# Spectral filter and Mish MLP on one core: low row parts turned by transposing transfers, w1 scaled in four parts, another order in the opening, a last tile in three pieces, joined row-0 products

## The chip, the core and the metric

The kernel runs on one core of a Trainium2 chip. The metric is the device time of one execution in microseconds. The core has TensorE (PE in the profile; its weight loads PEld), VectorE (DVE), ScalarE (ACT), GpSimd (POOL), and SyncE (SP), which issues the transfers. They run apart from each other, each through its own queue in order, and wait for each other by semaphores.

## The reference

```python
xn = layernorm(x)                                   # x: 2048 rows of 512, f32
h = xn @ w1 + b1                                    # w1: 512 x 1792
mlp = (h * tanh(softplus(h))) @ w2                  # mish; w2: 1792 x 512
X = rfft2(xn) * (w_r + 1j * w_i)                    # 2048 x 257 weights
out = x + irfft2(X, s=(2048, 512)) + mlp
```

## The kernel before

Every product runs on PE in f16 with each operand split into a high and a low f16 part: high·high, high·low and low·high, three matmuls (`mm3`, lines 61, 64, 65). ACT writes a high part, DVE mostly the low part as "source times scale minus high part".

The rows come in four groups of 512; a group is four tiles of 128 rows, "rows 0 to 3" of the opening being the tiles of group 0. For each tile, `hi` (ACT, line 178) writes the normalised high part into `xh`, `full` (DVE, 184) the normalised f32 row, and `lo` (DVE in group 0, POOL later, 194) the low part. Two things read `xh`: the row DFT (`s1_mm`, six matmuls of 256 columns into `psS`, whose output `s1_out` splits again, ACT line 97, DVE line 98), and a transposition into `xnT`, the moving operand of the MLP. In group 0 `turn_to` transposes on PE, four 128x128 blocks for one part of one tile, into a PSUM tile `pt`, and `place_from` copies `pt` to `xnT` (line 207, ACT or DVE). Groups 1 to 3 use `turn`, a transposing transfer of both parts of one tile from SP (line 198).

The MLP has 56 tiles: `up(n)` is 12 matmuls of 512 columns (line 639) into a PSUM bank `ph`, `mish(n)` the activation on ACT (650), `a_hi(n)` (ACT, 659) and `a_lo(n)` (DVE, 662) its split, and `down(n)` adds it into four banks `pa`. `ph` has two banks, tiles 2 and 3 stand in two others. Later tiles thus wait: `up(n)` for `mish(n-2)`. `mish` needs the tile's w1 scale (`exp_w1`), `a_hi` needs one activation scale (`act_scale`) for all tiles.

w1 arrives in seven blocks of 256 columns, each of 512 KB. Its power-of-two scales come from norms: `norm_w1(k)` on ACT (Square with a sum, 267) or DVE (a maximum, 271 and 272), `sum_w1(part)` an all-reduce across partitions on POOL (277), `scale_w1(part)` the small DVE operations behind it, then `w1_hi(k)` on ACT (291) and `w1_lo(k)` on DVE (295). `W1_PARTS` says which blocks share a scale: blocks 0, 1, and 2 to 6. The activation scale needs the scales of all parts and the largest entry of b1 (`bias_max`).

`opening` and `middle` are scheduled by hand: each engine executes its instructions in the order in which the code writes them. `opening` goes up to `up(13)`; in `middle` the `down` tiles of group 0 and the rows of the other groups interleave. After that the code interleaves the spectral stages with the remaining MLP tiles. In the spectral stage `spectrum(c, par)` multiplies by the weights on DVE and POOL; for par 0 it also makes the products of frequency row 0 by itself, on four partitions, from `g0` (two transferred rows) and `c0t`: three small DVE operations for each of two halves (lines 510 to 512). At the end, `end_of(s)` finishes the last group's four row tiles: nine matmuls for the last three MLP tiles, the final addition on DVE (733) and a store (734); the last row tile does so in two pieces of 256 columns. Transfers on SP use eight semaphores in turn, so that an issue can wait for the one eight places ahead.

```python
        for s in range(4):
            r.hi(s)
            r.full(s)
            r.lo(s, DVE)
```

Of the kernel before, what the change touches and what calls it, by code (L numbers as in the profile page):

```python
# [36 lines left out]
def spectral_mlp_kernel(ctx, tc, x, wt, w0, w1, b1, w2, cT, cIT, cM, out):  # L37
# [222 lines left out]
    def norm_w1(k, engine):  # L260
        part = min(k, 2)
# [27 lines left out]
    def w1_hi(k):  # L289
        fs = slice(2 * k * P, 2 * (k + 1) * P)  # L290
        nc.scalar.activation(w1t[:, 0, :, fs], w1st[k], AF.Copy, scale=sc["w1", min(k, 2)])

    def w1_lo(k):
# [4 lines left out]
            sc["w1", min(k, 2)],  # L298
# [172 lines left out]
    def spectrum(c, par):  # L471
# [157 lines left out]
    def up_parts(n, todo, by_block=False):  # L629
        for k in {t[0] for t in todo}:  # L630
# [6 lines left out]
        for i, ((k, hw, hx), dc) in enumerate(steps):  # L637
# [6 lines left out]
                stop=(hw, hx, dc) == todo[-1][1:] + (3,),  # L644
# [686 lines left out]
```

## Time and profile before

| | us |
|---|---|
| median of 3 runs | 373.07 (373.05 to 373.5) |
| the profiled execution | 373.23 |
| its span in the trace | 371.4 |
| outside the span | 1.83 |
| PE busy | 363.8 |
| DVE busy | 251.1 |
| ACT busy | 170.5 |
| POOL busy | 46.7 |

PE's granted clock is 1.00 in all of the span. Busy times are sums over instructions; matmuls are pipelined, so that the start-to-start distance of two is less than the duration of one. Times in a timeline count from the start of the span. A row that groups instructions shows the start of the first and the time to the end of the last. In brackets stands how long the engine had stood idle before the row, and what released it.

### The profile page before, as it was taken

Reading aid. Unit: us, or ns where it says so; the run is one execution under the profiler, and the core shown is the slowest. Engines: PE = TensorE matmul, PEld = TensorE weight load, DVE = VectorE, ACT = ScalarE, POOL = GpSimd, SP = SyncE. Lnnn points to the kernel's source line nnn. Section 1 sums busy time; section 2 is a strip of 40 time slices with the busy share of each in tenths; the row PEclk is TensorE's granted clock in tenths of the full one; section 3 lists DMA queues with packets and bytes.
Section 4 is the critical chain, followed back from the end, with each engine's and each line's share of the span. In section 5 each row is a group of like instructions: output and inputs, shape, how many; then the busy total and the mean of one; then the engine's idle time right before and its main releaser. Section 6 shows DMA issues by size and latency. Waiting matters only on the chain.

```text
span 371.4 us, 5642 instructions
## 1 busy us (share of the span) xinstructions
PE 363.8 (98%) x2084; PEld 185.7 (50%) x2084; DVE 251.1 (68%) x482; ACT 170.5 (46%) x257; POOL 46.7 (13%) x48
## 2 busy tenths in 40 slices
PE   8899999999999999999999999999999999999996
PEld 3544444544544455444555455544545445445564
DVE  4878998654467754599888866878479854424354
ACT  3889985424533533433544353445435344422100
POOL 0110003302203300203030303030030300000000
PEclk9999999999999999999999999999999999999999
DMA  8844921697665488035302361105921234449535
GB/s 272 271 140 151 326 64 28 177 323 245 191 178 123 104 222 271 15 115 222 119 2 64 104 188 45 41 25 163 299 99 44 62 95 106 122 94 338 218 151 192
DMA packets 55868, 55.79 MB, mean 150 GB/s; under 512 B 16112, under 2 KB 44560, under 8 KB 55072
## 3 DMA queue, kind: packets, MB, share of 16 engines
q1 hardware_dynamic: 55840, 55.43, 48.5%
q8 instruction: 16, 0.26, 0.3%
q14 instruction: 12, 0.10, 0.1%
HBM read 35.46 MB, written 12.58 MB: 129 GB/s over the span
## 4 chain that ended last, share of the span: by engine, by line
PE 88%; DVE 7%; DMA 2%; ACT 1%; issue 1%; SPq 0%; DVEq 0%; ACTq 0%
PE ph L639 36%; PE pa L64 12%; PE pa L65 12%; PE pa L61 12%; PE psP L454 1%; PE psT L61 1%; DMA x<-in_x_dram 1%; PE psY L61 1%; PE psY L65 1%; PE psP L464 1%; PE psY L64 1%; PE psT L65 1%; PE psT L64 1%; PE psS L65 1%; PE psS L61 1%; PE psS L64 1%
## 5 line engine op out<-in xcount | busy, mean ns | idle before, releaser
L639 PE MATMUL ph<-xnT,w1t 128*128 128x512 f16 x672 | 153.7, 379 | 0.0
L639 PEld LDWEIGHTS <-w1t 128*128 128x128 f16 x672 | 65.1, 98 | 74.0 <-issue 0.2
L650 ACT ACTIVATE hb<-ph,b1t,fp_exp 128x512 f32<-128x512 f32 x56 | 43.2, 773 | 78.2 <-PE ph L639 78.2
L65 PE MATMUL pa<-w2t,a 128*128 128x512 f16 x181 | 68.6, 379 | 0.0
L61 PE MATMUL pa<-w2t,a 128*128 128x512 f16 x181 | 68.6, 379 | 0.0
L64 PE MATMUL pa<-w2t,a 128*128 128x512 f16 x181 | 68.6, 379 | 0.0
L662 DVE SCALAR_TENSOR_TENSOR a<-hb,ip_a,a 128x512 f16<-128x512 f32 x46 | 35.9, 783 | 36.9 <-ACT a L659 36.8
L659 ACT ACTIVATE a<-hb,ip_a 128x512 f16<-128x512 f32 x46 | 32.9, 719 | 1.0
L65 PEld LDWEIGHTS <-a 128*128 128x128 f16 x187 | 18.3, 98 | 21.1
L61 PEld LDWEIGHTS <-a 128*128 128x128 f16 x187 | 18.3, 98 | 19.3
L64 PEld LDWEIGHTS <-a 128*128 128x128 f16 x187 | 18.3, 98 | 18.9
L194 POOL TENSOR_TENSOR xh<-xs,xh 128x512 f16<-128x512 f32 x12 | 15.7, 1307 | 62.8 <-ACT xh L178 32.9
L607 DVE SCALAR_TENSOR_TENSOR tt<-psT,tt 128x512 f16<-128x512 f32 x16 | 11.0, 687 | 16.8 <-ACT tt L606 16.8
L469 DVE SCALAR_TENSOR_TENSOR z<-psP,z 128x512 f16<-128x512 f32 x16 | 10.9, 690 | 13.4 <-ACT z L468 13.4
L178 ACT ACTIVATE xh<-x,nb,rs 128x512 f16<-128x512 f32 x16 | 12.7, 802 | 13.0 <-DVE nb L169 12.9
L363 ACT ACTIVATE u<-w,sc_u 128x512 f16<-128x512 f32 x16 | 10.8, 713 | 15.9 <-DVE w L560 7.4
L606 ACT ACTIVATE tt<-psT 128x512 f16<-128x512 f32 x16 | 9.5, 591 | 16.6 <-PE psT L65 13.9
L583 ACT ACTIVATE at<-psA 128x512 f16<-128x512 f32 x16 | 9.4, 586 | 13.1 <-PE psA L65 12.1
L468 ACT ACTIVATE z<-psP 128x512 f16<-128x512 f32 x16 | 9.5, 594 | 12.1 <-PE psP L464 12.1
L364 DVE SCALAR_TENSOR_TENSOR u<-w,sc_u,u 128x512 f16<-128x512 f32 x16 | 11.5, 749 | 5.0 <-ACT u L363 5.0
L98 DVE SCALAR_TENSOR_TENSOR y<-psS,y 128x512 f16<-128x512 f32 x16 | 10.9, 687 | 5.8 <-ACT y L97 5.8
L97 ACT ACTIVATE y<-psS 128x512 f16<-128x512 f32 x16 | 9.3, 589 | 12.0 <-PE psS L65 12.0
(204 smaller groups left out, 566.9 us busy)
## 6 DMA issues: line engine op xcount, KB each, us to landing
wm<-in_wt_dram SPq DMA_DIRECT2D x8, 512.0 KB
ai<-at SPq DMA_DIRECT2D x64, 64.0 KB
d_t<-tt SPq DMA_DIRECT2D x32, 128.0 KB
w1s<-in_w_dram SPq DMA_DIRECT2D x7, 512.0 KB
w2s<-in_w_dram SPq DMA_DIRECT2D x7, 512.0 KB
d_y<-y SPq DMA_DIRECT2D x7, 512.0 KB
m<-in_x_dram SPq DMA_DIRECT2D x3, 1024.0 KB
yt<-d_y SPq DMA_DIRECT2D x6, 512.0 KB
```

The lines of the kernel that those rows point to most:

```text
L61: first = nc.tensor.matmul(ps, stat(0), mov(0), start=start, stop=False)
L64: nc.tensor.matmul(ps, stat(0), mov(1), start=False, stop=False)
L65: nc.tensor.matmul(ps, stat(1), mov(0), start=False, stop=stop)
L98: nc.vector.scalar_tensor_tensor(y1v[:, :, 1, :], psv, 2.0**-17, y1v[:, :, 0, :], op0=ALU.mult, op1=ALU.subtract)
L178: nc.scalar.activation(xh[:, 0, :], self.x[s], AF.Identity, scale=self.rs[:, s : s + 1], bias=self.nb[:, s : s + 1])
L194: engine.tensor_sub(self.xh[s][:, 1, :], self.xs[s], self.xh[s][:, 0, :])
L364: nc.vector.scalar_tensor_tensor(dst_l, src, scale, dst_h, op0=ALU.mult, op1=ALU.subtract)
L607: nc.vector.scalar_tensor_tensor(tt[:, :, 1, :], ps, 2.0**-12, tt[:, :, 0, :], op0=ALU.mult, op1=ALU.subtract)
L639: nc.tensor.matmul(ph[n + k], w1t[:, hw, dc, f * P : (f + 1) * P], xnT[g][:, hx, dc, :], start=(hw, hx, dc) == (0, 0, 0), stop=(hw, hx, dc ...
L650: nc.scalar.activation(hbt[n], ph.pop(n), AF.Mish, bias=b1t[:, f : f + 1], scale=s_exp[part_of(f)])
L659: nc.scalar.activation(act[n][:, 0, :], hbt[n], AF.Copy, scale=sc["a"])
L662: nc.vector.scalar_tensor_tensor(act[n][:, 1, :], hbt.pop(n), sc["a"], act[n][:, 0, :], op0=ALU.mult, op1=ALU.subtract)
```

## The change

In the opening the low parts of rows 0 to 3 no longer go through PE. `turn_low` issues one transposing transfer of a low part on SP right behind `lo`. Half of the PE transposes and of the copies from `pt` go. Row 3's `full` and `lo` stand behind DVE's copies, its DFT products behind the first eight matmuls of `up(0)` and `up(1)`, and these two tiles do their high·low products last. w1 has four parts, blocks 0, 1, 2 to 3, and 4 to 6; block 2's norm moves from ACT to DVE, blocks 5's from DVE to ACT. The first `a_hi` stand together behind the activation scale, and some `s1_out` and `norm_w2` stand a few tiles later. In `end_of` the last row tile goes in pieces of 256, 128 and 128 columns. The row-0 products are three DVE operations of 4x256 elements instead of six of 4x128.

```diff
+        def turn_low(self, s):
+            to = self.xT[:, 1, :, s * P : (s + 1) * P]
+            nc.sync.dma_start_transpose(to, self.xh[s][:, 1, :])
...
-    W1_PARTS = [(0, 1), (1, 2), (2, 7)]
+    W1_PARTS = [(0, 1), (1, 2), (2, 4), (4, 7)]
...
             r0 = sp.tile([P, 2, 2, 64], F32, tag="r0", name=f"r0_{c}")
-            for a in range(2):
-                m2 = sp.tile([P, 2, 64], F32, tag="m2", name=f"m2_{c}_{a}")
-                nc.vector.tensor_mul(r0[q0, :, a, :], g0[q0, :, 0, :], c0t[q0, 2 * a])
-                nc.vector.tensor_mul(m2[q0], g0[q0, :, 1, :], c0t[q0, 2 * a + 1])
-                nc.vector.tensor_add(r0[q0, :, a, :], r0[q0, :, a, :], m2[q0])
+            m2 = sp.tile([P, 2, 2, 64], F32, tag="m2", name=f"m2_{c}")
+            for t, o in ((0, r0), (1, m2)):
+                nc.vector.tensor_mul(
+                    o[q0],
+                    g0[q0, :, t : t + 1, :].to_broadcast([4, 2, 2, 64]),
+                    c0t[q0, t::2].rearrange("g a r q -> g r a q"),
+                )
+            nc.vector.tensor_add(r0[q0], r0[q0], m2[q0])
...
-        w = D // 2 if s == 3 else D
-        for o in range(0, D, w):
+        for o, w in ((0, 256), (256, 128), (384, 128)) if s == 3 else ((0, D),):
             cs = slice(o, o + w)
-            ps = ps_h.tile([P, w], F32, tag="h", name=f"pe_{o}") if s == 3 else pa
+            pool, tag = (ps_f, "f") if o == 384 else (ps_h, "h")
+            ps = pool.tile([P, w], F32, tag=tag, name=f"pe_{o}") if s == 3 else pa
...
-        for s in range(4):
+        for s in range(3):
             r.hi(s)
             r.full(s)
             r.lo(s, DVE)
+            r.turn_low(s)
             if s == 1:
+                load_w1(4, w1_to[4])
                 norm_w1(0, ACT)
                 sum_w1(0)
-            if s == 2:
-                scale_w1(0)
...
+        r.hi(3)
...
+        ps1[2] = s1_bank(2, ps_a, "a")
+        s1_mm(2, r.xh[2], ps1[2])
+        r.place_from(pt_of(0), 0, 0, ACT)
+        scale_w1(0)
         w1_hi(0)
...
+        r.place_from(pt_of(1), 1, 0, DVE)
+        r.place_from(pt_of(2), 2, 0, DVE)
+        r.place_from(pt_of(3), 3, 0, DVE)
+        r.full(3)
+        r.lo(3, DVE)
+        r.turn_low(3)
+        nc.sync.dma_start(b1t, b1)
+        load_w1(5, w1_to[5])
+        load_w1(6, w1_to[6])
         norm_w1(1, ACT)
         sum_w1(1)
-        norm_w1(2, ACT)
         w1_lo(0)
+        norm_w1(2, DVE)
         scale_w1(1)
         exp_w1(0)
         w1_hi(1)
         norm_w1(3, ACT)
-        up_pair(0, (0, 1), (1, 0))
-        norm_w1(5, DVE)
+        sum_w1(2)
+        w1_lo(1)
+        up_parts(0, [(k, 0, 0) for k in range(2)], last=False)
+        ps1[3] = s1_bank(3, ps_a, "a")
+        s1_mm(3, r.xh[3], ps1[3])
+        up_parts(0, [(k, 1, 0) for k in range(2)], first=False, last=False)
+        up_parts(0, [(k, 0, 1) for k in range(2)], first=False)
         norm_w1(4, ACT)
...
+        mish(1)
+        norm_w1(5, ACT)
         norm_w1(6, DVE)
-        sum_w1(2)
...
+        sum_w1(3)
         up_pair(2, (0, 1), (1, 0))
+        mish(2)
+        w1_hi(3)
+        scale_w1(3)
         act_scale()
...
         mish(8)
         a_hi(8)
         a_lo(8)
-        norm_w2(3, ACT)
-        s1_out(3, ps1[3])
-        s1_store(3)
+        s1_out(2, ps1[2])
...
         up(10)
         mish(10)
+        s1_out(3, ps1[3])
+        s1_store(3)
```

DVE before, from row 3's `lo` to block 5's norm: the six copies from `pt` (first digit: rows 0, 1 or 2, 3; second: high or low part), `w1_lo(0)`, the second part's scale (`ip_w_1`) and a reduce for `qw_2`, the third part's norms.

```order
L194 TENSOR_TENSOR xh_191<-xs_193,xh_191 128x512 [waits DVE_49,Activation_49]
L207 COPY xnT_143<-pt_10_198 128x4x128 [waits PE_49]
L207 COPY xnT_143<-pt_10_198 128x4x128
L207 COPY xnT_143<-pt_01_197 128x4x128 [waits PE_49]
L207 COPY xnT_143<-pt_01_197 128x4x128
L207 COPY xnT_143<-pt_11_199 128x4x128 [waits PE_49]
L207 COPY xnT_143<-pt_11_199 128x4x128
L295 SCALAR_TENSOR_TENSOR w1t<-w1s_125,ip_w_0_188,w1t 128x4x256 [waits DMAHW3_49,Activation_49]
L230 TENSOR_SCALAR ip_w_1_276<-qs_271 128x1 [waits Pool_49]
L233 TENSOR_SCALAR ip_w_1_276<-ip_w_1_276 128x1 [waits DVE_49]
L239 TENSOR_SCALAR fp_exp_279<-ip_w_0_188 128x1
L271 TENSOR_REDUCE qw_2_273<-w1s_136 128x1 [waits DMAHW1_49]
```

Row 3's `lo`, the first row here, and three of the six copies leave this place.

DVE now, from the first copy to the second part's scale: `pt_h` holds rows 0 and 1, `pt_a` rows 2 and 3, the reduce for `qw_2` is block 2's norm.

```order
L211 COPY xnT_139<-pt_h 128x4x128 [waits Activation_49]
L211 COPY xnT_139<-pt_a 128x4x128 [waits PE_49]
L211 COPY xnT_139<-pt_a 128x4x128
L184 TENSOR_SCALAR xs_237<-x_121,mv_136,rs_137 128x512
L194 TENSOR_TENSOR xh_188<-xs_237,xh_188 128x512 [waits DVE_49]
L302 SCALAR_TENSOR_TENSOR w1t<-w1s_125,ip_w_0_230,w1t 128x4x256 [waits DMAHW3_49,Activation_49]
L278 TENSOR_REDUCE qw_2_249<-w1s_127 128x1 [waits DMAHW5_49]
L279 SCALAR_TENSOR_TENSOR qw_2_249<-qw_2_249 128x1 [waits DVE_49]
L234 TENSOR_SCALAR ip_w_1_252<-qs_246 128x1 [waits Pool_49]
L237 TENSOR_SCALAR ip_w_1_252<-ip_w_1_252 128x1 [waits DVE_49]
```

Three copies went, row 3's `full` and `lo` moved from ahead of the copies to behind them, a norm stands between `w1_lo(0)` and the second scale, and the first copy waits for ACT.

ACT before, from block 1's norm (`qw_1`) to the first `a_hi`: norms go into `qw`, high parts of w1 have `ip_w` as an operand, `hb` is a `mish`.

```order
L267 ACTIVATE w1t,qw_1_269<-w1s_127 128x4x256 [waits DMAHW4_49]
L267 ACTIVATE w1t,qw_2_273<-w1s_129 128x4x256 [waits DMAHW5_49]
L291 ACTIVATE w1t<-w1s_127,ip_w_1_276 128x4x256 [waits DVE_49,Activation_49]
L267 ACTIVATE w1t,qw_2_273<-w1s_131 128x4x256 [waits DMAHW6_49]
L267 ACTIVATE w1t,qw_2_273<-w1s_134 128x4x256 [waits DMAHW0_49]
L650 ACTIVATE hb_0_316<-ph_0_283,b1t,fp_exp_279 128x512 [waits DMAHW7_49,DVE_49,PE_49]
L650 ACTIVATE hb_1_328<-ph_1_284,b1t,fp_exp_279 128x512 [waits PE_49]
L291 ACTIVATE w1t<-w1s_129,ip_w_2_332 128x4x256 [waits DVE_49,Activation_49]
L650 ACTIVATE hb_2_374<-ph_2_335,b1t,fp_exp_323 128x512 [waits PE_49]
L659 ACTIVATE a_0_376<-hb_0_316,ip_a 128x512 [waits DVE_49,Activation_49]
```

The second row, block 2's norm, leaves ACT.

ACT now, over the same stretch; part 2 (`ip_w_2`) is blocks 2 and 3, `qw_3` the norms of blocks 4 to 6.

```order
L274 ACTIVATE w1t,qw_1_244<-w1s_126 128x4x256 [waits DMAHW4_49]
L298 ACTIVATE w1t<-w1s_126,ip_w_1_252 128x4x256 [waits DVE_49,Activation_49]
L274 ACTIVATE w1t,qw_2_249<-w1s_128 128x4x256 [waits DMAHW6_49]
L274 ACTIVATE w1t,qw_3_295<-w1s_129 128x4x256 [waits DMAHW1_49]
L661 ACTIVATE hb_0_299<-ph_0_262,b1t,fp_exp_255 128x512 [waits DMAHW4_49,DVE_49,PE_49]
L298 ACTIVATE w1t<-w1s_127,ip_w_2_303 128x4x256 [waits DMAHW5_49,DVE_49]
L661 ACTIVATE hb_1_318<-ph_1_263,b1t,fp_exp_255 128x512 [waits PE_49]
L274 ACTIVATE w1t,qw_3_295<-w1s_130 128x4x256 [waits DMAHW5_49]
L661 ACTIVATE hb_2_351<-ph_2_325,b1t,fp_exp_297 128x512 [waits PE_49]
L298 ACTIVATE w1t<-w1s_128,ip_w_2_303 128x4x256 [waits Activation_49]
L661 ACTIVATE hb_3_370<-ph_3_326,b1t,fp_exp_297 128x512 [waits PE_49]
L670 ACTIVATE a_0_373<-hb_0_299,ip_a 128x512 [waits DVE_49,Activation_49]
```

A norm moved in behind `mish(1)`, `mish(0)` stands ahead of the third scale's first use, and `a_hi(0)` moved from behind `mish(2)` to behind `mish(3)`.

SP before, from the load of w1's third block on; `b1t` is the bias.

```order
L257 DMA w1s_129<-in_w_dram 128x4x256
L257 DMA w1s_131<-in_w_dram 128x4x256
L873 DMA b1t<-in_b_dram 128x14
L257 DMA w1s_134<-in_w_dram 128x4x256 [waits DMAHW0_49]
L257 DMA w1s_136<-in_w_dram 128x4x256 [waits DMAHW1_49]
L257 DMA w1s_136<-in_w_dram 128x4x256 [waits DMAHW2_49]
```

The bias and the last three loads move back.

SP now, from the same block on.

```order
L264 DMA w1s_127<-in_w_dram 128x4x256
L264 DMA w1s_128<-in_w_dram 128x4x256
L202 DMA_TRANSPOSE xnT_139<-xh_165 128x4x128 [waits DVE_49]
L202 DMA_TRANSPOSE xnT_139<-xh_171 128x4x128 [waits DMAHW0_49,DVE_49]
L264 DMA w1s_129<-in_w_dram 128x4x256 [waits DMAHW1_49]
L202 DMA_TRANSPOSE xnT_139<-xh_182 128x4x128 [waits DMAHW2_49,DVE_49]
L202 DMA_TRANSPOSE xnT_139<-xh_188 128x4x128 [waits DMAHW3_49,DVE_49]
L928 DMA b1t<-in_b_dram 128x14 [waits DMAHW4_49]
L264 DMA w1s_130<-in_w_dram 128x4x256 [waits DMAHW5_49]
L264 DMA w1s_130<-in_w_dram 128x4x256 [waits DMAHW6_49]
```

Four transposing transfers stand among the loads, and the bias and blocks 5 and 6 behind the last of them.

## Rows read from the trace of the kernel before

**Rows 1.** Stretches: us, busy PE PEld DVE ACT POOL (count), clock, DMA, GB/s

```profile
0.00:16.22 16.22, 12.79 (x80) 6.95 (x81) 10.33 (x31) 10.02 (x15) 1.39 (x8) 1.00 0.93 304
48.00:368.10 320.10, 319.26 (x1858) 164.33 (x1856) 212.42 (x402) 131.08 (x199) 43.39 (x38) 1.00 0.46 138
```

**Rows 2.** PE's waits: line, releaser, us in total, times, longest

```profile
PE dim L61 <- DVE at L584: 0.4, 1, 0.4
```

**Rows 3.** PE's timeline in the opening: start us, us, engine, line, operation

```profile
13.09 0.62 PE L202 MATMUL pt<-cTt,xh 128*128 128x128 f16 x8 [0.31 <-ACT xh L178]
13.54 0.27 PE L61 MATMUL psS<-xh,cTt 128*128 128x256 f16 x1
...
14.20 0.87 PE L202 MATMUL pt<-cTt,xh 128*128 128x128 f16 x8
...
16.22 36.47 PE L639 MATMUL ph<-xnT,w1t 128*128 128x512 f16 x168
```

**Rows 4.** Timeline of ACT in the opening

```profile
12.94 1.04 ACT L207 COPY xnT<-pt 128x512 f16<-128x512 f16 x2
...
18.15 1.15 ACT L291 ACTIVATE w1t<-w1s,ip_w 128x1024 f16<-128x1024 f32 x1 [1.03 <-DVE fp_exp L239]
19.20 1.04 ACT L267 ACTIVATE w1t<-w1s 128x1024 f16<-128x1024 f32 x1
...
23.33 1.15 ACT L291 ACTIVATE w1t<-w1s,ip_w 128x1024 f16<-128x1024 f32 x1 [0.62 <-DVE ip_w L233]
25.06 0.78 ACT L650 ACTIVATE hb<-ph,b1t,fp_exp 128x512 f32<-128x512 f32 x1 [0.58 <-PE ph L639]
25.73 0.71 ACT L659 ACTIVATE a<-hb,ip_a 128x512 f16<-128x512 f32 x1
...
33.27 0.78 ACT L650 ACTIVATE hb<-ph,b1t,fp_exp 128x512 f32<-128x512 f32 x1
34.08 0.72 ACT L659 ACTIVATE a_z<-hb,ip_a 128x512 f16<-128x512 f32 x1
...
43.47 0.57 ACT L97 ACTIVATE y<-psS 128x512 f16<-128x512 f32 x1
...
46.41 0.76 ACT L650 ACTIVATE hb<-ph,b1t,fp_exp 128x512 f32<-128x512 f32 x1
```

**Rows 5.** Timeline of DVE in the opening

```profile
13.28 0.54 DVE L184 TENSOR_SCALAR xs<-x,mv,rs 128x512 f32<-128x512 f32 x1
...
14.54 2.07 DVE L207 COPY xnT<-pt 128x512 f16<-128x512 f16 x6
16.52 1.28 DVE L295 SCALAR_TENSOR_TENSOR w1t<-w1s,ip_w,w1t 128x1024 f16<-128x1024 f32 x1
17.72 0.15 DVE L230 TENSOR_SCALAR ip_w<-qs 128x1 int32<-128x1 int32 x1
...
18.03 1.21 DVE L271 TENSOR_REDUCE qw<-w1s 128x1 f32<-128x1024 f32 x1
...
22.70 0.16 DVE L283 TENSOR_REDUCE qt<-qs 128x1 f32<-128x5 f32 x1 [0.35 <-POOL qs L277]
...
24.18 0.14 DVE L239 TENSOR_SCALAR fp_exp<-ip_w 128x1 int32<-128x1 int32 x1
```

**Rows 6.** POOL's timeline in the opening: the third part's sum, five columns

```profile
21.47 1.20 POOL L277 PARTITION_ALL_REDUCE qs<-qw  x1 [4.91 <-ACT w1t L267]
```

**Rows 7.** Timeline of SP's issues in the opening: the bias

```profile
4.63 2.85 SPq L873 DMA_DIRECT2D b1t<-in_b_dram  x1
```

**Rows 8.** Chain that ended last, its start: start us, us, what

```profile
0.72 3.72 DMA x<-in_x_dram
```

**Rows 9.** Line 198, transposing issues of whole tiles: ns min/median/max

```profile
L198 SPq DMA_TRANSPOSE xnT<-xh x12: 1233/1241/2772, 61.3 to 135.2; - x12
```

**Rows 10.** Tile r, row-0 products: ns min/median/max

```profile
L510 DVE TENSOR_TENSOR r<-g,c0t x8: 271/278/289, 159.2 to 276.9; 4x128 f32<-4x128 f32 x8
```

**Rows 11.** Line 733, the last tile's additions: ns min/median/max

```profile
L733 DVE SCALAR_TENSOR_TENSOR y<-pe,s_out,y x2: 484/484/485, 367.1 to 368.1; 128x256 f32<-128x256 f32 x2
```

More of the change, by code (lines that the diff above doesn't have):

```diff
@@ L248, in spectral_mlp_kernel, with w1_part @@
     sc = {}
-    W1_PARTS = [(0, 1), (1, 2), (2, 7)]
+    W1_PARTS = [(0, 1), (1, 2), (2, 4), (4, 7)]
     w1st, w1q = {}, {}
+    def w1_part(k):
+        return next(i for i, (a, b) in enumerate(W1_PARTS) if a <= k < b)
     def part_of(f):
-        return min(f // 2, 2)
+        return w1_part(f // 2)
     def load_w1(c, t):
@@ L260, in norm_w1 @@
     def norm_w1(k, engine):
-        part = min(k, 2)
+        part = w1_part(k)
         a, b = W1_PARTS[part]
@@ L290, in w1_hi @@
         fs = slice(2 * k * P, 2 * (k + 1) * P)
-        nc.scalar.activation(w1t[:, 0, :, fs], w1st[k], AF.Copy, scale=sc["w1", min(k, 2)])
+        nc.scalar.activation(w1t[:, 0, :, fs], w1st[k], AF.Copy, scale=sc["w1", w1_part(k)])
     def w1_lo(k):
@@ L297, in w1_lo @@
             w1st.pop(k),
-            sc["w1", min(k, 2)],
+            sc["w1", w1_part(k)],
             w1t[:, 0, :, fs],
@@ L627, in up_pair, with up_parts @@
         up_parts(n, [(k, 0, 0) for k in range(2)] + [(k,) + p for k in range(2) for p in (second, third)])
-    def up_parts(n, todo, by_block=False):
-        for k in {t[0] for t in todo}:
+    def up_parts(n, todo, by_block=False, first=True, last=True):
+        for k in {t[0] for t in todo} if first else ():
             g, f = UP[n + k]
@@ L643, in up_parts @@
                 start=(hw, hx, dc) == (0, 0, 0),
-                stop=(hw, hx, dc) == todo[-1][1:] + (3,),
+                stop=last and (hw, hx, dc) == todo[-1][1:] + (3,),
             )
@@ L863, in opening @@
         load_ct(0)
+        w1_to = {}
         for c in range(7):
@@ L870, in opening @@
                 t = tu[:, c - 5]
-            load_w1(c, t)
-            if c == 3:
-                nc.sync.dma_start(b1t, b1)
+            w1_to[c] = t
+        for c in range(4):
+            load_w1(c, w1_to[c])
         r = Rows(0, [x0[:, s, :] for s in range(4)])
@@ L931, in opening @@
         norm_w1(3, ACT)
-        up_pair(0, (0, 1), (1, 0))
-        norm_w1(5, DVE)
-        norm_w1(4, ACT)
-        norm_w1(6, DVE)
-        sum_w1(2)
-        mish(0)
-        bias_max()
-        exp_w1(1)
-        act_min()
-        w1_lo(1)
-        mish(1)
-        scale_w1(2)
+        sum_w1(2)
[5 more added lines that the diff above has]
+        up_parts(0, [(k, 0, 1) for k in range(2)], first=False)
+        norm_w1(4, ACT)
+        exp_w1(1)
+        mish(0)
+        scale_w1(2)
+        w1_hi(2)
+        exp_w1(2)
+        act_min()
+        bias_max()
+        w1_lo(2)
+        mish(1)
+        norm_w1(5, ACT)
+        norm_w1(6, DVE)
+        sum_w1(3)
         up_pair(2, (0, 1), (1, 0))
+        mish(2)
+        w1_hi(3)
+        scale_w1(3)
         act_scale()
-        exp_w1(2)
-        w1_hi(2)
-        w1_lo(2)
-        mish(2)
+        exp_w1(3)
+        mish(3)
+        w1_lo(3)
         a_hi(0)
         a_lo(0)
-        w1_hi(3)
-        mish(3)
         a_hi(1)
         a_lo(1)
-        w1_lo(3)
         a_hi(2)
@@ L968, in opening @@
         a_lo(3)
-        a_hi(4)
-        a_lo(4)
         w1_hi(4)
@@ L976, in opening @@
         up(5)
-        s1_out(0, ps1[0])
-        s1_out(1, ps1[1])
-        s1_store(1)
         mish(5)
+        a_hi(4)
+        a_lo(4)
         a_hi(5)
@@ L987, in opening @@
         mish(6)
-        s1_out(2, ps1[2])
         a_hi(6)
         a_lo(6)
+        s1_out(0, ps1[0])
+        s1_out(1, ps1[1])
+        s1_store(1)
+        up(7)
+        mish(7)
         norm_w2(1, ACT)
         norm_w2(2, DVE)
-        up(7)
-        mish(7)
         a_hi(7)
@@ L1012, in opening @@
         mish(9)
+        norm_w2(3, ACT)
         a_hi(9)
```

36 lines of the change are left out of this document (9 added, 27 removed).

## The prediction

> **What bounds the kernel now.** I read the view of stretches first. From 48 us to 368.1 us PE is busy 319.26 of 320.10 us [rows 1]: whatever starts that stretch earlier or later moves the end by as much, and another engine matters there only where PE waits. The list of PE's waits has one place in it that the change touches, 0.4 us on DVE near 290 us [rows 2]. PE's timeline then gives the ledger on which this change works [rows 3]: row transposes and row DFT products up to 16.22 us, and from there `up` tiles without a gap, each 12 matmuls of 512 columns; 168 of them make 36.47 us, so one pitch is (36.47 − 0.38)/167 = 0.2161 us and a tile 2.593 us. `up(12)` thus starts at 16.22 + 12 x 2.593 = 47.34 us. ACT, in its timeline [rows 4], is the nearest other bound: `mish(10)`, whose bank `up(12)` takes, ends at 46.41 + 0.76 = 47.17 us, 0.17 us before PE asks for it. So PE sets the opening's end with ACT right behind it, and what PE saves pays only if ACT comes forward as well.
>
> **Opening on PE.** Sixteen of 32 transposes go. Eight cost 0.45 us (13.09 to 13.54) and the six products of a row 0.66 us (13.54 to 14.20) [rows 3]. Row 3's high part still starts at 13.09 and takes four transposes (0.22), then rows 1 and 2 take 1.32: PE is ready for `up(0)` at 14.63 instead of 16.22. Row 3's products (0.66) now stand inside `up(0)`, so PE's work up to `up(12)` shrinks by 1.59 − 0.66 = 0.93 us.
>
> **What `up(0)` needs.** ACT copies row 0 from 12.94, one of two that took 1.04, to 13.46, then `w1_hi(0)` takes 1.15 [rows 4]: 14.61, no wait. DVE's first copy now waits for ACT's of the same bank, 13.46, and with it two copies and `full` and `lo` of row 3 that are queued behind it. Three copies at 2.07/6 = 0.34 end at 14.5; `full` and `lo` took 14.54 − 13.28 = 1.26 [rows 5], so 15.76, in time for row 3's products near 16.4. `w1_lo(0)`, 17.72 − 16.52 = 1.20 [rows 5], ends at 16.96, just when its matmuls are due, 14.65 + 8 x 0.216 + 0.66 = 17.04.
>
> **The turned low parts.** The last is issued at 15.8 and read from 17.04 + 8 x 0.216 = 18.77: 2.9 us may pass. A transposing issue of twice the size takes 1.24 us in the median and 2.77 at most [rows 9]; a load of 512 KB held the chain for 3.72 us [rows 8]. These bound the landing between 1.2 and 2.77 + 3.72 = 6.5 us. I take 2.5, nearer to the lower end, because 128 KB move, a quarter of that load, and so no wait; the upper end is rival D.
>
> **ACT's ledger,** which decides. DVE, after `w1_lo(0)` at 16.96, does `norm_w1(2)` (1.21 [rows 5] and a short operation, 1.3) ahead of scale 1, and from the start of that scale to `w1_hi(1)` it took 18.15 − 17.72 = 0.43 [rows 4, 5]: `w1_hi(1)` starts at 18.7, not 18.15. From there to `mish(10)` ACT took 46.41 − 18.15 = 28.26 us. What changes in that stretch:
> - one more norm on ACT (block 5, from DVE): +1.04 [rows 4];
> - `s1_out(3)`, 0.57 [rows 4], goes behind `mish(10)`: −0.5, as it overlaps its neighbour a little;
> - the idle 0.62 (scale of the third part) and 0.58 (waiting for PE) at 23.33 and 25.06 [rows 4] go, because a `mish` stands ahead of that scale now and PE is earlier: −1.2;
> - `a_hi` stands right behind its own `mish` twice (6, 8) instead of four times (5, 7, 8, 9): start to start that took 34.08 − 33.27 = 0.81 against 25.73 − 25.06 = 0.67 where it belongs to another [rows 4]: −0.3;
> - a new idle ahead of `a_hi(0)`, which needs the activation scale and thus part 3's sum. ACT gets there after three `w1_hi`, three norms and four `mish`: 18.7 + 6 x 1.05 + 4 x 0.7 = 27.8. DVE's `norm_w1(6)` stands behind `w1_lo(2)`, which follows `w1_hi(2)`; that ends at 18.7 + 4 x 1.05 + 0.7 = 23.6, `w1_lo(2)` at 24.8, the norm at 26.1. POOL's sum took 1.20 for five columns [rows 6]; for three I take 0.8, between 0 and 1.20. The small DVE operations from the reduce to the scale took 24.18 − 22.70 = 1.48 [rows 5], with the hops at either end 1.8. So the scale comes at 28.7: +0.9.
>
> The sum is 1.04 − 0.5 − 1.2 − 0.3 + 0.9 = −0.06. With the late start of 0.55 `mish(10)` begins 0.5 late, at 46.9, and ends at 47.67: `up(12)` starts at 47.7 instead of 47.34, **+0.35 us**, and PE's 0.93 us are waited away for `ph` banks on the way. Ends: −0.5, if POOL's sum costs nothing and the new idle shrinks to 0.1; +1.0, if it takes 1.20 and nothing is saved on `a_hi`.
>
> **Other moves.** The fourth part adds an all-reduce on POOL, which idles there, and small DVE operations that lie in the time costed above. The other `s1_out` and the second layer's norms move by a tile or two but stay ahead of `mish(10)`, and their readers come behind `up(12)`: 0. Without that cover each would cost ACT 0.57 or 1.04.
>
> **Row-0 products.** Four times six DVE operations of 0.278 [rows 10] become three of twice the width, at 0.28 to 0.56 each; I take the middle, 0.42. A chain saves 1.67 − 1.26 = 0.4 us, but only the last of the four feeds a wait of PE, of 0.4 [rows 2], and between it and that wait DVE also stands for ACT's activations. I take −0.15 (0 to −0.4).
>
> **Last tile.** The last DVE operation took 0.484 for 256 columns [rows 11]; for 128 it costs between 0.24 and 0.484, and I take 0.35, −0.13. PE's 18 matmuls of 128 columns instead of nine of 256 move the same columns, and eight transposes of 128 took 0.056 each [rows 3], so nothing there. The final store halves, −0.07: 64 KB less are 0.2 us at the 304 GB/s of the first stretch [rows 1], and at least part of a store is not bytes. Together −0.2 (−0.4 to +0.1, if short rows in a store cost more).
>
> **Sum.** 371.4 + 0.35 − 0.15 − 0.2 = 371.4 us of span, and 1.83 around it as in the profiled execution: 373.23. The median lies 0.16 below that execution, so the forecast is **373.1 us**: no change. A measurement of this kernel tells 0.2%, 0.75 us, from nothing.
>
> **Rivals.** *B, faster: ACT keeps pace* and PE's 0.93 us survive: 373.07 − 0.93 − 0.35 = 371.8; with two thirds of it 372.1. For it: ACT loses 1.2 us of idle [rows 4]. Against: the activation scale must come 1.3 us sooner than worked out, with a norm, a sum and eight small operations in one row ahead of it. It decides at `mish(8)`: done by 41.3 us, `up(10)` doesn't wait.
>
> *C, slower: SP is late with w1's last blocks.* b1's issue, 2.85 [rows 7], and blocks 5 and 6 now stand behind the turned part of row 3. With the dear issue of 2.77 [rows 9], block 5 is issued at 15.8 + 2.77 + 2.85 = 21.4 and lands 3.72 later, 25.1; block 6, 1.7 us of bytes behind it at 304 GB/s [rows 1], at 26.8. `norm_w1(6)` wants it at 24.8. Scale and ACT come 2.0 us later: 375.1. With the median issue and a short b1 issue, block 6 lands at 23 to 25 and costs nothing; this is why the case is near.
>
> *D, slower: the turned rows are late.* With the dear issue and the whole chain of a load, 2.77 + 3.72 = 6.5 us [rows 8, 9], row 3's part arrives at 22.3 and PE waits 3.5 us. What PE waits there it no longer waits for ACT's banks, so without another gap the time is 373.07 + 3.5 − 0.93 − 0.35 = 375.3; it is slower by over 0.2% from a landing of 5 us on (373.8). Against it: a quarter of that load's bytes. The Trainium skill, "VectorE: DVE Perf Modes", speaks against the edit: its section "Rules for kernel authors" wants TensorE for a 128x128 transpose where PSUM will do, and "The three transpose paths" gives 1309 ns for one by DMA. Four in a row would be an estimate of 5.2 us, a wait of 2.3 and a time of 374.1 instead of 373.1; eight squares are issued in 1.24 us here [rows 9], which speaks against one after the other, but no row here shows such a short transfer's landing.
>
> *E: the change does not do what it says,* the low parts reach PE no earlier and nothing else moves; then only the last tile and the row-0 products count, 372.7, within no change.
>
> **Chances.** No change 0.52 (E in it; own range 372.4 to 373.8), B 0.25, C 0.15, D 0.08. So faster by over 0.2% 0.25, within it 0.52, slower 0.23. The range goes from B whole, 371.8, to most of C, 374.8; about one in ten is left out on either side.
>
> **What would show it.** Right: `up(0)` at 14.65 in PE's timeline, `w1_hi(1)` at 18.7, an idle of about 0.9 us on ACT ahead of `a_hi(0)` released by DVE, waits of PE for ACT of about 1.3 us together within `up(4)` to `up(11)`, `up(12)` at 47.7, a last DVE operation of 0.35 us. Wrong: ACT stands less than 0.3 us ahead of `a_hi(0)` (B); the last norm of w1 waits for a load (C); the third group of `up(0)` waits for a DMA (D); or PE waits in the last stretch for something that no view of before shows.

## The result, and the profile after

The changed kernel took 374.05 us in the median of 15 runs (373.55 to 375.31), beside 373.5 us (373.05 to 374.32) for the kernel before on the same chips. The ratio is 1.0018, 95% interval 1.001 to 1.0027: about 0.7 us slower, at the edge of the 0.2% that the prediction set as its bound. The profiled execution took 374.58 us with a span of 372.8, against 371.4 before.

The page's busy times and the granted clock of PE in 40 slices, after:

```profile
PE 363.6 (98%) x2077; PEld 185.3 (50%) x2077; DVE 250.0 (67%) x473; ACT 169.6 (45%) x256; POOL 46.0 (12%) x49
...
PEclk9899999999999999999999999999999999999999
```

All engines have a little less to do than before, and the span is longer. One digit of the clock is not 9. By the microsecond (stretch, length, then busy us and count of PE, PEld, DVE, ACT, POOL, then the clock):

```profile
11.00:12.00 1.00, 1.00 (x8) 0.51 (x5) 0.90 (x3) 1.00 (x3) 0.17 (x1) 0.64 0.78 245
12.00:13.00 1.00, 0.65 (x5) 0.35 (x4) 0.90 (x2) 1.00 (x2) 0.42 (x1) 0.50 1.00 146
13.00:14.00 1.00, 0.91 (x8) 0.73 (x8) 0.80 (x5) 1.00 (x3) 0.00 (x0) 0.50 0.68 127
14.00:15.00 1.00, 1.00 (x8) 0.78 (x7) 1.00 (x4) 1.00 (x2) 0.00 (x0) 0.66 0.31 37
```

For three microseconds PE ran at 1.2 instead of 2.4 GHz. Its timeline there, to be held against [rows 3]:

```profile
10.00 0.40 PE L206 MATMUL pt_h<-cTt,xh 128*128 128x128 f16 x4 [1.81 <-ACT xh L178]
...
12.45 1.31 PE L206 MATMUL pt_a<-cTt,xh 128*128 128x128 f16 x8 [0.35 <-ACT xh L178]
13.55 0.42 PE L61 MATMUL psS<-xh,cTt 128*128 128x256 f16 x1
...
15.42 1.89 PE L650 MATMUL ph<-xnT,w1t 128*128 128x512 f16 x8
```

PE stood for 1.81 us ahead of its first row transpose (0.95 in the first trace of before); a product of 256 columns then took 0.42 us instead of 0.27, and `up(0)` began at 15.42, not at 14.65.

ACT's timeline in the opening, to be held against [rows 4]:

```profile
18.75 1.15 ACT L298 ACTIVATE w1t<-w1s,ip_w 128x1024 f16<-128x1024 f32 x1 [3.03 <-DVE fp_exp L243]
...
28.52 1.95 ACT L670 ACTIVATE a<-hb,ip_a 128x512 f16<-128x512 f32 x3 [0.77 <-DVE fp_exp L243]
...
46.71 0.77 ACT L661 ACTIVATE hb<-ph,b1t,fp_exp 128x512 f32<-128x512 f32 x1
```

DVE's row for block 6's norm, which didn't wait for the load:

```profile
24.91 1.21 DVE L278 TENSOR_REDUCE qw<-w1s 128x1 f32<-128x1024 f32 x1
```

POOL's for the sum over three columns, to be held against [rows 6]:

```profile
26.49 0.43 POOL L284 PARTITION_ALL_REDUCE qs<-qw  x1 [3.26 <-DVE qw L279]
```

SP's issue of the bias, to be held against [rows 7]:

```profile
17.14 0.57 SPq L928 DMA_DIRECT2D b1t<-in_b_dram  x1
```

And the view of line 202, the four turned low parts (ns min/median/max), half the size of those of [rows 9]:

```profile
L202 SPq DMA_TRANSPOSE xnT<-xh x4: 1188/1195/1317, 10.7 to 15.9; - x4
```

These are the forecast's steps, to within 0.2 us: `w1_hi(1)` at 18.75 (18.7 forecast), 0.77 us of ACT idle ahead of `a_hi(0)` (0.9), released by DVE, and `mish(10)` at 46.71 (46.9). `down(0)`, two tiles behind `up(12)`, started at 52.70 us against 52.53 before.

So the opening accounts for 0.17 us. The rest came later. PE's timeline after 48 us, the rows that wait:

```profile
79.53 2.76 PE L650 MATMUL ph<-xnT,w1t 128*128 128x512 f16 x12 [0.73 <-DMA xnT<-xh]
...
290.76 0.39 PE L61 MATMUL dim<-z,cMt 128*128 128x512 f16 x1 [0.21 <-DVE at L595]
...
316.51 0.38 PE L61 MATMUL psT<-ai,cMt 128*128 128x512 f16 x1 [0.56 <-DVE tt L618]
...
337.28 0.28 PE L61 MATMUL psY<-yi_z,cITt 128*128 128x256 f16 x1 [0.52 <-DMA yi_z<-d_t]
```

Before had two waits here, 0.43 at `dim` and 0.23 at `psY`, and none at 79 and 316. The number in brackets counts from the modelled end of the matmul before. A matmul of 512 columns has a duration of 0.38 us, but the next one follows 0.22 us after its start, so measured from start to start such a wait costs 0.16 us more: 0.90 us at 79. That wait is `up(14)` standing for the last turned row of group 1, which landed at 79.48 (landings are read from the completion marks of a transfer in the trace). In the first trace of before the same row landed at 77.50, 0.96 us ahead of `up(14)` at 78.46. Start against start, PE was behind the first trace by 0.17 us at 52.7, 1.07 at 79.5, 0.86 at 290.8, 1.39 at 316.5 and 1.67 at 337.3. From the start of the last DVE operation to the end of the span it was 372.8 − 369.82 = 2.98 us instead of 371.4 − 368.12 = 3.28.

### The profile page after: what moved, and what is told of

It reads as the page before. It is cut to its first block, busy times and chain, and to the rows that moved or that the text cites. A ratio compares the mean times of both kernels' runs of the same rounds, so it can differ in the third digit from the quotient of the medians.

```text
span 372.8 us, 5632 instructions
## 1 busy us (share of the span) xinstructions
PE 363.6 (98%) x2077; PEld 185.3 (50%) x2077; DVE 250.0 (67%) x473; ACT 169.6 (45%) x256; POOL 46.0 (12%) x49
## 4 chain that ended last, share of the span: by engine, by line
PE 72%; DVE 11%; ACT 6%; DMA 5%; issue 2%; SPq 2%; POOL 0%; ACTq 0%; DVEq 0%; POOLq 0%
PE ph L650 28%; PE pa L65 10%; PE pa L64 10%; PE pa L61 10%; DMA xnT<-xh 2%; DVE w1t L302 1%; DVE st L121 1%; DVE q L345 1%; DVE w2t L366 1%; PE psP L462 1%; DMA x<-in_x_dram 1%; PE psY L61 1%; ACT w1t L298 1%; PE psP L472 1%; PE psY L64 1%
## 5 line engine op out<-in xcount | busy, mean ns | idle before, releaser
L65 PEld LDWEIGHTS <-a 128*128 128x128 f16 x190 | 18.6, 98 | 21.0
L61 PEld LDWEIGHTS <-a 128*128 128x128 f16 x190 | 18.6, 98 | 19.3
L64 PEld LDWEIGHTS <-a 128*128 128x128 f16 x190 | 18.6, 98 | 18.9
```

The costliest lines, as they stand in the source:

```text
L61: first = nc.tensor.matmul(ps, stat(0), mov(0), start=start, stop=False)
L64: nc.tensor.matmul(ps, stat(0), mov(1), start=False, stop=False)
L65: nc.tensor.matmul(ps, stat(1), mov(0), start=False, stop=stop)
```

## The experiments

Each ratio is to the kernel before, run beside it. Where a diff is against the changed kernel or the one before is said.

**Each kernel again** (no edit), for a second trace.

> The changed kernel once more. Theory A, the lost time sits in waits behind the opening that belong to the change: in the new trace PE again waits about 0.7 us for a turned row of group 1 near 79.5 us, and down(0) starts within 0.3 us of 52.7. Rival, that wait is an accident of one execution: PE is gapless there and the profiled time is nearer to 373.6 than to 374.6. PE's granted clock fell to 0.5 from about 11.2 to 14.6 us in the first trace; if ACT decides the opening, down(0) starts at 52.7 with the fall or without it.

> The kernel before once more, for a second trace. If the wait of PE near 79 us lies in the kernel before as well and the first trace only fell on its good side (a transposing issue of 2.77 us), the issue takes over 4 us here and PE waits 0.3 to 0.7 us. Rival: the wait comes with the change, and PE is gapless again up to 290 us. The ratio is 1.000 within 0.001, which says how far these comparisons can be trusted.

The changed kernel: 374.17 us, 1.0016 (1.0004 to 1.0027). The kernel before: 373.49 us, 0.9999 (0.9988 to 1.001), so these comparisons hold to about 0.1%. Of the changed kernel, the clock stayed at 0.5 beyond 16 us this time, ACT waited for PE, and `down(0)` came at 53.86, more than a microsecond late: ACT decides the opening only while the clock fall is short. PE was so late that its list of waits has none at 79 us. But the chain that ended last goes through the turned row's transfer there (start us, us, what):

```profile
73.28 6.71 DMA xnT<-xh
```

It landed at 79.99 and released `up(14)`, which came 0.24 us later than the usual distance of two matmuls. The second trace of before has a clock fall too (0.5 from 12 to 14 us, after PE had stood 1.94 us) and `down(0)` at 53.03. What it was to show, a long issue and a wait at 79, it didn't: the longest issue took 2.84 us, and the row landed at 78.44, 0.53 us ahead of `up(14)`. So the fall is not the changed kernel's alone; how often it comes has to be counted.

For the clock every run gives a number, its mean over the span: 0.998 to 1.000, 0.994 to 0.995, or 0.991 (two runs of one experiment have 0.997). Counted over the runs of before beside the experiments and over both sets of the changed kernel, with their mean times:

| kernel | near 1.0 | near 0.995 | 0.991 |
|---|---|---|---|
| before, three sets, 104 runs | 79: 373.52 us | 25: 374.03 us | none |
| changed, two sets, 27 runs | 11: 373.87 us | 11: 374.20 us | 5: 374.94 us |

A quarter of the runs of before have the fall and well over half of the changed kernel's, some of them the long one; why it falls more often there no run shows. Over all runs the two differ by 374.20 − 373.64 = 0.56 us, over runs near full clock by 0.35. The clock is 0.2 us of the difference.

**A longer start for PE.** Both kernels begin with 24 matmuls on zeros whose result nobody reads (`warm`), so that PE is busy before the first rows arrive. On the changed kernel:

```diff
-        warm(24)
+        warm(32)
```

> The changed kernel with 32 instead of 24 idle matmuls of 512 columns at the start, so that PE does not stand for 1.5 to 1.8 us ahead of its first row transpose. Theory: most of the loss against the kernel before is the granted clock that falls from 1.0 to 0.5 at about 11.2 us in many executions of the changed kernel, and it falls after that stand. Then the clock stays at 1.0 in the opening, no execution shows a mean clock of 0.991, and the median falls by 0.4 to 0.6 us against the changed kernel. Rival: ACT decides the opening with or without the fall, and the median stays within 0.2 us.

373.96 us, 1.0008 (0.9998 to 1.0017), 0.2 us below the changed kernel's second set, and the clock near 1.0 in all 12 runs. Over the five kernels with 32 idle matmuls no run of 57 fell. The theory of the clock holds in that the longer start removes the fall. Over the 14 traces, the clock fell in the four in which PE had stood 1.36 to 1.94 us ahead of its first transpose, and in none in which it had stood 0 to 1.24. In these four the 24 idle matmuls had ended at 8.14 to 8.43 us, in the five others with 24 at 8.45 to 9.54; early end and long stand go together, and the traces can't part them. The size was smaller than expected, and 0.44 us above the mean of before near full clock (373.56 in that set) are still there. With the clock at 1.00, `up(0)` started at 14.53 and PE waited for ACT as forecast: 0.56 us by its list of waits, 1.03 us from start to start up to `down(0)`. Two rows of its waits (line, releaser, us in total, times, longest):

```profile
PE psY L61 <- DMA yi_z<-d_t: 1.6, 1, 1.6
...
PE ph L650 <- ACT hb L661: 0.6, 2, 0.4
```

`down(0)` started at 52.48. At full clock the opening is thus neither better nor worse than before (52.53, 52.28 with tail and row 0 alone). The turned row landed at 78.58 and released `up(14)` 0.22 us late, too little for the list. The loss of this execution sits further on: at 311 us PE was level with the first trace of before (0.04 us ahead), at `psY` near 336 us it was 1.4 behind.

**The parts apart.** Tail and row 0 on the kernel before, with these two hunks; and the new opening alone, the changed kernel with the same two hunks taken back.

```diff
-            for a in range(2):
-                m2 = sp.tile([P, 2, 64], F32, tag="m2", name=f"m2_{c}_{a}")
...
+            m2 = sp.tile([P, 2, 2, 64], F32, tag="m2", name=f"m2_{c}")
+            for t, o in ((0, r0), (1, m2)):
...
-        w = D // 2 if s == 3 else D
-        for o in range(0, D, w):
+        for o, w in ((0, 256), (256, 128), (384, 128)) if s == 3 else ((0, D),):
```

> The kernel before with only the tail in three pieces and the joined row-0 products. From the traces the tail gave 0.29 us and the wait before dim shrank by 0.21, so theory A expects 0.5 us less than before, a ratio of 0.9987, and no wait of PE near 79 us. Rival, what row 0 gives is waited away at the next psT: 0.3 us less, a ratio of 0.9992.

> The new opening alone on the kernel before: tail in two pieces, row-0 products as before. If the parts add, it is 1.2 us slower than before (the whole change +0.6, tail and row 0 alone -0.6), a ratio of 1.003. Rival: the opening itself costs 0.35 us by ACT as worked out, a ratio of 1.001, and the rest is scatter.

Tail and row 0: 372.98 us, 0.9984 (0.9975 to 0.9993). New opening alone: 374.42 us, 1.0022 (1.0011 to 1.0034). The parts add within their intervals: 0.6 us gained, 0.8 lost. What was expected of PE in the first wasn't there: it waited 0.55 us near 79 us with the old opening too, as the turned row landed at 78.83. That trace is of the slowest of the twelve runs (373.74 us), so the wait need not be the usual case. The same with 32 idle matmuls:

> The opening of before with the tail in three pieces, the joined row-0 products and 32 idle matmuls instead of 24. About a third of the executions of before show a mean clock of 0.995 and lie 0.5 us higher, so if the longer idle work removes them, the mean falls by 0.15 us against tail and row 0 alone: a ratio of 0.998 to before, and no clock below 0.998. Rival: eight more matmuls delay the first row transposes, and the time is 0.3 us higher than tail and row 0 alone, 0.999.

373.37 us, 0.9985 (0.9974 to 0.9995): the same ratio again, clock near 1.0 in all 11 runs; in its trace the turned row landed at 77.59, 0.68 us ahead of `up(14)`. These two have the lowest ratios measured, and both beat both kernels (one further down, 0.9988, can't be told from them); the longer start adds nothing that can be told from scatter.

PE's timeline in the trace of the new opening alone, with a clock of 1.00 throughout, shows where its loss is (1.34 us from start to start; the span is 1.4 us longer than in the first trace of before):

```profile
79.85 2.76 PE L647 MATMUL ph<-xnT,w1t 128*128 128x512 f16 x12 [1.17 <-DMA xnT<-xh]
```

`down(0)` had started at 52.58.

**Who holds the turned row at 79 us?** On SP the two loads of group 2's rows are issued right ahead of the last two turned rows of group 1. The edit puts them behind (on the changed kernel; later also with scale 1 ahead of block 2's norm and 32 idle matmuls, and on tail and row 0 alone):

```diff
-        x2 = load_rows(2)
         down(5)
         row_turn(r, 2)
         w2_part(5)
         down(6)
         row_turn(r, 3)
+        x2 = load_rows(2)
```

> The changed kernel with the loads of group 2's rows issued behind the last two turned rows of group 1 instead of ahead of them. If the turned row was late because its issue stood behind those loads' bytes, the transposing issues there take about 1.24 us instead of 4.7, PE's wait near 79.5 goes, and the time falls by 0.7 us against the changed kernel. Rival, the rows of group 2 then come about 4 us later, DVE stands before their statistics and PE waits for it: no gain, or 0.5 us lost.

373.64 us, 1.0005 (0.9995 to 1.0016), 0.5 us below the changed kernel run beside it, with overlapping intervals; no wait at 79 us, as the row landed at 75.98. Part of the 0.5 is the clock, which fell in 5 of these 12 runs and in 8 of the 12 beside them. Near full clock the mean is 373.57 us (7 runs), beside 373.64 in that set of the changed kernel (4 runs) and 373.87 in both sets (11). So the move gives 0.1 to 0.3 us there, not the 0.7 expected. The view of line 198 tells what became of the issues (ns min/median/max), of the changed kernel:

```profile
L198 SPq DMA_TRANSPOSE xnT<-xh x12: 1232/1242/4708, 61.5 to 136.3; - x12
```

And with the late loads:

```profile
L198 SPq DMA_TRANSPOSE xnT<-xh x12: 1231/1248/2053, 61.3 to 135.5; - x12
```

The longest fell to 2.05 us, not to 1.24. SP's rows for the last two turned rows of group 1 show what the wait at 79 is made of, of before:

```profile
71.29 4.12 SPq L198 DMA_TRANSPOSE xnT<-xh  x2
```

And of the changed kernel:

```profile
71.23 6.21 SPq L198 DMA_TRANSPOSE xnT<-xh  x2
```

The two are issued at the same time and SP is done with them 2.0 us later, and by as much later the row lands (1.9 to 2.3 us behind the end of its issue in all ten traces). It isn't PE that comes early. With the new opening and these loads in front the row landed at 78.42 to 79.99 in all six traces and released `up(14)` each time, which cost 0.22 to 1.34 us from start to start. With the old opening it landed at 77.50 to 78.83, and PE waited in one trace of four.

Behind two 512 KB loads the issue of a turned row takes far more than 1.24 us. Over the traces with these loads in front the longest took 2.77, 2.84, 3.40 and 4.33 us with the opening of before, and 4.15, 4.22, 4.43, 4.64, 4.71 and 5.17 with the new one. Why it is longer behind the new opening no run shows; the SP rows right ahead of it differ only in that the two loads were issued in 1.75 to 1.76 us in all six, and in 1.75 to 2.63 in the four.

**What if ACT no longer holds PE back?** Scale 1 first (changed kernel):

```diff
-        norm_w1(2, DVE)
         scale_w1(1)
         exp_w1(0)
+        norm_w1(2, DVE)
```

> The changed kernel with scale 1 ahead of block 2's norm on DVE. If ACT's chain decides the opening, w1_hi(1) starts at 17.4 instead of 18.75, a_hi(0) near 27.2 instead of 28.52, and down(0) at 51.8 instead of 52.7: 0.9 us less than the changed kernel at most, 0.5 if PE's clock falls again. Rival, part 2's scale (block 2's norm now later) takes the place: a_hi(0) stays within 0.3 us of 28.5 and the time within 0.3 us of the changed kernel.

373.46 us, 1.0001 (0.9987 to 1.0015), 0.7 us below the changed kernel beside it, though the clock fell in 6 of its 12 runs. Near full clock it took 373.05 us in the mean, beside 373.40 of before in that set: there part of the gain arrives. ACT came forward: `w1_hi(1)` at 17.16 and `a_hi(0)` at 27.90. The latter was expected near 27.2; DVE stood for the load of block 6, ahead of the last norm:

```profile
24.28 1.22 DVE L278 TENSOR_REDUCE qw<-w1s 128x1 f32<-128x1024 f32 x1 [0.87 <-DMA w1s<-in_w_dram]
```

So `down(0)` came forward less, to 52.06. And at 79 us the lead was gone in this execution, in PE's timeline:

```profile
79.10 2.76 PE L650 MATMUL ph<-xnT,w1t 128*128 128x512 f16 x12 [0.94 <-DMA xnT<-xh]
```

This is the mechanism that the prediction lacked: 0.47 us won in the opening against before, 0.94 waited at 79 (1.11 from start to start), as the turned row landed at 79.05, 1.55 us later than in the first trace of before. With 32 idle matmuls, and then with the loads late as well:

> The changed kernel with scale 1 ahead of block 2's norm and 32 idle matmuls. ACT then no longer holds PE back and the clock stays up, so down(0) starts near 52.0, 0.5 us earlier than in the first trace of before. If PE then waits near 79 us for the turned row, as it did with scale 1 first alone (0.94 us), that gain is taken back there and the time is 373.2 beside 373.7 of before, a ratio of 0.999, from the tail and row 0 alone. Rival: the opening's gain arrives, 0.9975.

> The same with the loads of group 2's rows behind the last turned row of group 1. If the wait near 79 us is what takes the opening's gain back, it goes, and the time is 0.5 us or more below the run without that move: a ratio of 0.9975. Rival: the later loads cost the same elsewhere (waits for the stored spectral rows near 336 us, or the last stores, which took 1 us longer in the run of the old opening with this move), and the ratio is 0.999 or above.

373.49 us, 0.9995 (0.9987 to 1.0004), `down(0)` at 52.01 and a wait of 0.36 at 79; then 373.07 us, 0.9988 (0.9978 to 0.9999), `down(0)` at 51.57 and no wait there. The step between the two is 0.3 to 0.4 us, with overlapping intervals; the direction is that of the theory. But in the traces 0.44 us of it is there at `down(0)` already, ahead of the loads that were moved: DVE waited 0.74 us for block 6 in the first, whose trace is of its slowest run (374.13 us), and not at all in the second. So the step isn't shown to be the move's. And the second falls short of the 0.9975 expected. Its PE is 0.96 us ahead of before at `down(0)` and at 314 us, and then waits, by the list of its waits:

```profile
PE psY L61 <- DMA yi_z<-d_t: 1.1, 1, 1.1
```

There the spectral branch goes through DRAM, a store and a load with nothing between. The chain of waits at this place (start us, us, what), of before:

```profile
330.26 2.44 DMA d_t<-tt
332.81 2.75 DMA yi_z<-d_t
```

And of the changed kernel with 32 idle matmuls:

```profile
330.26 3.71 DMA d_t<-tt
334.11 2.85 DMA yi_z<-d_t
```

The load takes 2.6 to 2.9 us in every trace. The store took 2.44 to 2.65 in all but the four traces that have both the new opening and 32 idle matmuls (2.85, 3.34, 3.37, 3.71). Whether this is those kernels' own or chance, four traces can't say; it stays open.

**Two that went wrong.** Block 6's norm ahead of `w1_lo(2)`, to bring the activation scale forward, with the three edits above:

```diff
-        w1_lo(2)
         mish(1)
         norm_w1(5, ACT)
         norm_w1(6, DVE)
         sum_w1(3)
+        w1_lo(2)
```

> The changed kernel with 32 idle matmuls, scale 1 ahead of block 2's norm, block 6's norm ahead of w1_lo(2), and the loads of group 2's rows behind the last turned row of group 1. If ACT's chain, the clock and the wait near 79 us are the three costs, a_hi(0) starts near 26.6 instead of 28.5, down(0) at 51.6, 0.9 us earlier than in the kernel before, no wait near 79 us, and the time is 1.2 to 1.5 us below the kernel before. Rival: one of them comes back later (DVE behind the norm of block 6, the turned rows of group 2), and the gain over the tail and row-0 changes alone (0.6) is under 0.2.

373.94 us, 1.0004 (0.9994 to 1.0014). DVE's timeline shows it standing for the load:

```profile
24.51 1.22 DVE L278 TENSOR_REDUCE qw<-w1s 128x1 f32<-128x1024 f32 x1 [3.09 <-DMA w1s<-in_w_dram]
```

And PE's shows it standing for `w1_lo(2)`, which is queued behind that norm:

```profile
27.18 13.12 PE L650 MATMUL ph<-xnT,w1t 128*128 128x512 f16 x60 [0.86 <-DVE w1t L302]
```

Block 6 landed at 24.49 us here, and at 23.1 to 24.3 in the eight other traces of the new opening. The changed kernel asks for it at 24.91; over the five traces with its order there, 0.4 to 2.1 us were left. A second cost stands on POOL, whose sum over three columns took 0.43 us in the changed kernel:

```profile
26.09 1.32 POOL L284 PARTITION_ALL_REDUCE qs<-qw  x1 [4.21 <-ACT w1t L298]
```

On DVE the moved `w1_lo(2)` ran beside it:

```profile
25.84 1.28 DVE L302 SCALAR_TENSOR_TENSOR w1t<-w1s,ip_w,w1t 128x1024 f16<-128x1024 f32 x1
```

In the eight other traces with three columns DVE did nothing during this sum, and it took 0.43 us each time. So `a_hi(0)` came at 29.02, where 26.6 was expected, and `down(0)` at 53.19.

The late loads on tail and row 0 alone:

> The opening of before, with the tail in three pieces, the joined row-0 products, and the loads of group 2's rows behind the last turned row of group 1. If the wait of PE near 79 us (0.55 in the run of tail and row-0 alone) is there in most executions, the time is about 0.4 us under that run: 372.6 beside 373.6 of before. Rival: that wait is given back at later waits for DMA, and it stays at 373.0.

374.39 us, 1.0015 (1.0005 to 1.0025), 1.4 us above tail and row 0 alone. Not on PE: `up(14)` didn't wait, and PE ended earlier than there. DVE's last addition:

```profile
368.47 0.35 DVE L736 SCALAR_TENSOR_TENSOR y<-pe,s_out,y 128x128 f32<-128x128 f32 x1 [0.15 <-PE pe L65]
```

The span ends at 372.4, 3.93 us after the start of this row; with tail and row 0 alone that was 372.0 − 368.89 = 3.11 us (spans are given to 0.1 us). The last store was slower by 0.8 us: fifteen of its sixteen completion marks had come by 370.49, the last came at 371.40. The changed kernel with late loads (2.97) doesn't show it, so it isn't the move as such. Its cause wasn't found, nor where the rest of the 1.4 us lies.

## Why the prediction was right, and where it wasn't

The forecast was 373.1 us, no change, between 371.8 and 374.8. The measured 374.05 lies in that range. It lies outside the narrower 372.4 to 373.8 of the likeliest case, of which 0.43 us are the kernel before, which itself took 373.5 in these runs instead of 373.07. In the ratio it is 0.1 to 0.27% slower, where the forecast had 0 and a bound of 0.2%. That it fell in the range is partly luck: the opening came out better than forecast, costs that the sum had put at nothing came on top, and the range was made wide for rivals B and C, neither of which came about.

By its terms: the opening came out at 0 instead of +0.35, row 0 and the tail at −0.21 and −0.16 instead of −0.15 and −0.2. That would make 0.4 us faster. The means over all runs differ by +0.56, of which the clock is 0.2. So about 0.7 us are left for what lies behind the opening, which the prediction had put at nothing. From start to start the traces show 0.90 and 0.24 us lost at 79 us in the changed kernel's two, and 1.34 in the new opening alone. Near full clock the late loads gave back only 0.1 to 0.3 us, so that the rest lies at 79 is not shown; the waits at 316 and 337 us differ from trace to trace, and with the longer start 1.4 us were lost at the latter.

- **ACT decides the opening: right.** The steps of the ledger came as worked out. The term furthest off was POOL's sum over three columns: 0.43 us, not 0.8; the steps around it took 0.2 us more, so the new idle was 0.77 instead of 0.9, and `down(0)` at full clock stood at 52.5 where +0.35 would have been 52.9. Reading POOL's time from its columns was the mistake: two took 0.46, one 0.39, and three took 1.32 with `w1_lo(2)` beside them on DVE. The five columns of before, 1.20, had a `w1_lo` beside them too, in all five traces. That ACT is the cause was shown by putting scale 1 first, with 32 idle matmuls on both sides: `w1_hi(1)` came 1.3 us earlier (17.23 for 18.53), `a_hi(0)` and `down(0)` 0.5 us. In the trace where block 6 also came in time `down(0)` was 0.9 us earlier, at 51.57, and PE didn't wait for ACT at all.
- **Waits of 1.3 us for ACT in `up(4)` to `up(11)`: a little too many.** At full clock 1.03 us from start to start (0.56 by the list of waits). In the profiled execution, where the clock had eaten most of PE's lead, 0.37, and none by the list.
- **The clock: missed.** The one trace of before showed 1.00 throughout, and the prediction took it as given. It cost 0.2 us in the mean, and more than 1 us in the runs with a mean clock of 0.991.
- **"Whatever starts that stretch earlier or later moves the end by as much": wrong.** This was the first step, read from PE being busy 319.26 of 320.10 us. A row without a wait says nothing of how near the next one is. The turned row that `up(14)` reads had landed 0.96 us ahead of it in the first trace of before and 0.53 in the second; the issue of this row took 1.3 to 2.4 us longer with the new opening than in these two, and that was more than they had left. Where the new opening had a lead, it was lost there or, further on, to the `d_t` store and the `yi` load ahead of 336 us.
- **Row-0 products, −0.15: right.** The wait before `dim` went from 0.43 (also 0.44 and 0.43 in other traces with the old products) to 0.21 or 0.22 in all with the joined ones.
- **Last tile, −0.2: right.** From the last addition to the end 3.28 us in both traces of before, 3.11 and 3.14 with the pieces and the old opening (3.93 in the one with the late store). The last operation took 0.35 us as forecast. Part of the 0.30 in the changed kernel isn't the pieces': the new opening with the old tail stands at 3.04.
- **"Other moves: 0": wrong,** together with the step on PE. What SP does 50 us later wasn't weighed.
- **Rival B** (PE's 0.93 survives) did not come about; even with ACT out of the way it would have met the wait at 79. **Rival C** (w1's last blocks late) did not come about in the changed kernel's order, by 0.4 to 2.1 us, but its wait came as soon as ACT's chain was shorter: 0.87 and 0.74 us for block 6 with scale 1 first. b1's issue took 0.57, not 2.85. **Rival D** (turned rows late) did not: `lo(3)` ended at 15.6 with scale 1 first, the third group was read at 18.6 and didn't wait, so the landing took less than 3.0 us. It was near: row 3's part landed at 18.36 there, and at 18.78 with the new opening alone, where the third group began at 18.87, 0.1 us late. The sentence on the Trainium skill ("VectorE: DVE Perf Modes", "The three transpose paths") made 5.2 us of four squares one after the other; the trace does not agree with that use of it.

## What to carry to other kernels

A gapless engine isn't slack-free ahead: look for the transfers that land just ahead of its reads (the issue time of each, what stands in front of it on its queue, and how long before the read it lands: here 0.5 to 1 us, less than the issue times differ), for they take back what an earlier stage gives. When a change takes work from PE in an opening that waits for other engines, look at the granted clock of several executions, and pay with idle matmuls up to the first real one. Measure the parts of a joint change apart: here 0.6 us of gain (tail and row 0) were in it, under 0.8 us of loss.

## What the runs showed of the hardware

- A transposing issue of 128x512 takes 1.19 us and one of 128x1024 1.24 us: halving the bytes saves hardly any of SP's time. Behind two loads of 512 KB the larger one took 2.77 to 5.17 us (ten traces), and its row landed 1.9 to 2.3 us after the issue's end.
- The clock fell from 2.4 to 1.2 GHz at 11 to 12 us only in those traces in which PE had stood 1.36 us or longer ahead of the first transpose, for 3 to 7 us; the mean clock of a run (1.000, 0.995, 0.991) tells which runs had it.
- POOL's sum across partitions over three columns took 0.43 us in eight traces, with DVE idle, and 1.32 us in the one with a DVE operation of 128x1024 elements (`w1_lo(2)`) beside it for 1.03 us. It isn't every such neighbour: a sum over one column took 0.39 us with the start of a `w1_lo` beside it.
- One final store took 0.8 us longer in one trace, with the same code at that place: the last of its sixteen completion marks came 0.9 us behind the others. All runs of that kernel took long (373.99 us at the least); that each of them had this late mark is not shown.
